# Sliding-window attention beside a gated MLP: the order of the first chunk's transposes and V projections

## The chip, the cores and the metric

The kernel runs on one core of a Trainium2 chip. The metric is the device time of one execution in microseconds, lower is better. The engines are called PE (matrix multiply; PEld is its weight load, which overlaps it), DVE (vector), ACT (scalar, activations), POOL and SP (here only an issuer of DMAs).

## The reference

For x of shape (1, 2048, 512), all in bf16:

```python
xn = _layernorm(x)                              # (x - mean) / sqrt(var + 1e-5) over the 512
return x + _A_ref(xn, wqkv, wo) + _B_ref(xn, w_gate, w_up, w_down)

# _A_ref: 32 heads of 16; each query sees itself and the 255 keys before it
qkv = (xn @ wqkv).reshape(B, S, 3, H, Dh)
p = softmax(where(mask, q @ k.T * Dh ** -0.5, -1e9))
A = (p @ v) @ wo
# _B_ref: F = 1792
B = ((xn @ w_gate) * (xn @ w_up)) @ w_down
```

## The kernel before

The 2048 rows are worked on in four chunks T of four blocks of 128 rows. For a chunk, the rows are normalised (`norm_stats`, `norm_scale`, `norm_apply`), transposed so that the 512 inputs lie on the partitions (`norm_transpose`, tile `xnT`, four groups of 128 inputs, index k), and projected to V (`proj_v`, L243), to Q and K (`proj_qk`, L255) and to gate and up (L399, L410). Scores (L317), exponentials (L323), masks, P times V (L370), the down projection and Wo follow, and the gate, up and down matmuls of one chunk are spread by `run` between the attention steps. The program writes out the order of every engine by hand: each engine runs its instructions in the order in which `run` records them, and waits on semaphores where it needs another's result.

The change touches what happens before that steady part. `setup` issues the loads on SP in a written order: x of blocks 0, 1 and 2 to 3, then `Wqkv` in three DMAs (the V columns, then K, then Q), then `Wg`, `Wu`, x of blocks 4 to 7, the second halves of `Wg` and `Wu`, `Wd`, `Wo`, and x of the blocks left. Then `keep_busy(40)` puts 40 matmuls of zeros (tile `wps`, L131) on PE.

`first_chunk` normalises chunk 0. DVE computes the statistics (L173, L174), POOL the inverse root (L186), DVE scales a block to `xn` (L194). PE transposes the block's four 128x128 parts (L213) into a PSUM tile `xTp`, and ACT copies that to `xnT` (L214): for block 0 in two PSUM tiles of two parts, each copied by itself, for the other blocks in one tile of four parts and one copy. `proj_v(b)` is four matmuls of 128x512 that sum over k into one PSUM bank `vp`; DVE or ACT then copies it to V (L236, L234). `ps_m` is a pool of four PSUM banks, from which `xTp`, `vp`, `qkp` and also the idle matmuls take theirs.

PE's order in the first chunk is: the transposes of block 0, eight idle matmuls, the transposes of block 1, the V sum of block 0, the transposes of block 2, the V sum of block 1, the transposes of block 3, the V sums of blocks 2 and 3, and then the first K, Q and K sums (L255). So each block's transposes stand one whole V sum ahead of the sum that reads them.

Of the kernel before, what the change touches and what calls it, by code (L numbers as in the profile page):

```python
# [8 lines left out]
F32 = mybir.dt.float32  # L9
I32 = mybir.dt.int32  # L10
ACT = mybir.ActivationFunctionType
ALU = mybir.AluOpType
# [22 lines left out]
class Kernel:  # L35
# [26 lines left out]
    def setup(self):  # L62
        nc, const, NT, NF = self.nc, self.const, self.NT, self.NF
        self.x = const.tile([128, NT, 512], BF16, name="x")
        self.Wqkv = const.tile([128, 4, 1536], BF16, name="Wqkv")
        self.Wo = const.tile([128, 4, 512], BF16, name="Wo")
        self.Wg = const.tile([128, 4, self.F], BF16, name="Wg")
        self.Wu = const.tile([128, 4, self.F], BF16, name="Wu")
        self.Wd = const.tile([128, NF, 512], BF16, name="Wd")
        xv = self.x_d.rearrange("(t p) d -> p t d", p=128)  # L70
        wq = self.w_d["qkv"].rearrange("(k p) n -> p k n", p=128)
        wg = self.w_d["g"].rearrange("(k p) n -> p k n", p=128)
        wu = self.w_d["u"].rearrange("(k p) n -> p k n", p=128)
        for lo, hi in ((0, 1), (1, 2), (2, 4)):
            nc.sync.dma_start(out=self.x[:, lo:hi, :], in_=xv[:, lo:hi, :])
        for lo in (1024, 512, 0):
            nc.sync.dma_start(out=self.Wqkv[:, :, lo:lo + 512], in_=wq[:, :, lo:lo + 512])
        h = self.F // 2
        for lo in (0, h):
            nc.sync.dma_start(out=self.Wg[:, :, lo:lo + h], in_=wg[:, :, lo:lo + h])  # L80
            nc.sync.dma_start(out=self.Wu[:, :, lo:lo + h], in_=wu[:, :, lo:lo + h])
            if lo == 0:
                nc.sync.dma_start(out=self.x[:, 4:8, :], in_=xv[:, 4:8, :])
        nc.sync.dma_start(out=self.Wd[:], in_=self.w_d["d"].rearrange("(f p) n -> p f n", p=128))
        wo = self.w_d["o"].rearrange("(c p) n -> p c n", p=128)
        for c in range(4):
            nc.sync.dma_start(out=self.Wo[:, c, :], in_=wo[:, c, :])
        for lo, hi in ((8, 10), (10, 12), (12, NT)):
            nc.sync.dma_start(out=self.x[:, lo:hi, :], in_=xv[:, lo:hi, :])

        warm = const.tile([128, 1], F32, name="warm")
        nc.vector.memset(warm[:], 0.0)
        nc.scalar.activation(out=warm[:], in_=warm[:], func=ACT.Exp)
        self.idle = const.tile([128, 128], BF16, name="idle")
        nc.vector.memset(self.idle[:], 0.0)
        self.keep_busy(40)
        ident = const.tile([128, 128], BF16, name="ident")
        nc.gpsimd.memset(ident[:], 0.0)
        nc.gpsimd.affine_select(out=ident[:], in_=ident[:], compare_op=ALU.not_equal, fill=1.0,
                                base=0, pattern=[[-1, 128]], channel_multiplier=1)  # L100
        self.ident = ident
        pi = const.tile([128, 1], I32, name="pi")
        nc.gpsimd.iota(pi[:], pattern=[[0, 1]], base=0, channel_multiplier=1)
        podd = const.tile([128, 1], I32, name="podd")
        nc.vector.tensor_scalar(out=podd[:], in0=pi[:], scalar1=4, scalar2=1,
                                op0=ALU.arith_shift_right, op1=ALU.bitwise_and)
        self.odd = const.tile([128, 1], F32, name="odd")
        nc.vector.tensor_copy(out=self.odd[:], in_=podd[:])
        self.even = const.tile([128, 1], F32, name="even")
        nc.vector.tensor_scalar(out=self.even[:], in0=self.odd[:], scalar1=-1.0, scalar2=1.0,  # L110
                                op0=ALU.mult, op1=ALU.add)
        self.mhalf = const.tile([128, 4], F32, name="mhalf")
        nc.gpsimd.memset(self.mhalf[:], -0.5)
        self.diag = const.tile([128, 64], BF16, name="diag")
        self.far = const.tile([128, 64], BF16, name="far")
        nc.gpsimd.memset(self.diag[:], BIG)
        nc.gpsimd.memset(self.far[:], BIG)
        for half in (slice(0, 64), slice(64, 128)):
            self.triangle(self.diag[half], True)
            self.triangle(self.far[half], False)  # L120
        self.xnT, self.Q, self.hT, self.OT = {}, {}, {}, {}
        self.K, self.V, self.VS = {}, {}, {}
        self.strips, self.parts, self.at = {}, {}, {}
        self.stock = []
        self.new_values()

    def keep_busy(self, n):

        ps = self.ps_m.tile([128, 128], F32, tag="M", name="wps")
        for _ in range(n):  # L130
            self.nc.tensor.matmul(ps[:], lhsT=self.idle[:], rhs=self.idle[:], start=True, stop=True)  # L131

    def new_chunk(self, T):

# [55 lines left out]
    def norm_apply(self, t):  # L190
        nc = self.nc
        mv, j, rs = self.stats.pop(t)
        xn = self.work.tile([128, 512], BF16, tag="xn", name="xn")
        nc.vector.tensor_scalar(out=xn[:], in0=self.x[:, t, :], scalar1=mv[:, j, 0:1],  # L194
                                scalar2=rs[:, j:j + 1], op0=ALU.subtract, op1=ALU.mult)
        self.book("dve", MASK)
        self.xns[t] = xn

    def norm_transpose(self, t, by_dma):

        nc = self.nc
        xn = self.xns.pop(t)
        T, b = divmod(t, 4)
        if b == 0:
            self.xnT[T] = self.chunk2.tile([128, 4, 4, 128], BF16, tag="xnT", name=f"xnT{T}")
        if by_dma:
            nc.sync.dma_start_transpose(out=self.xnT[T][:, b, :, :], in_=xn[:])
            return
        n = 2 if b == 0 else 4
        for lo in range(0, 4, n):  # L210
            ps = self.ps_m.tile([128, n, 128], BF16, tag="M", name="xTp")
            for k in range(n):
                nc.tensor.transpose(ps[:, k, :], xn[:, 128 * (lo + k):128 * (lo + k) + 128], self.ident[:])  # L213
            nc.scalar.activation(out=self.xnT[T][:, b, lo:lo + n, :], in_=ps[:], func=ACT.Copy)  # L214

    def bank(self, ks, name):

# [54 lines left out]
    def first_chunk(self):  # L272

        self.new_chunk(0)
        for b in range(2):
            self.norm_stats(b, 1)
            self.norm_scale(b, 1)
        for b in (0, 1, 2):
            self.norm_apply(b)
            if b < 2:  # L280
                self.norm_stats(b + 2, 1)
                self.norm_scale(b + 2, 1)
        self.norm_transpose(0, False)
        self.keep_busy(8)
        for b in range(4):
            if b < 3:
                self.norm_transpose(b + 1, False)
            self.proj_v(b, engine="act" if b == 2 else "dve")
            if b == 0:
                self.norm_apply(3)  # L290
        self.proj_qk(0, 0, 1, engine="dve")
        self.proj_qk(0, 0, 0, engine="act")
        self.swap_halves(0, self.nc.scalar)
        self.proj_qk(0, 1, 1, engine="dve")
# [234 lines left out]

    def run(self):  # L530
        self.xns, self.stats, self.sums = {}, {}, {}
        self.pads = 0
        self.now, self.free = 0, dict(act=0, dve=0)
        self.setup()
        NCH = self.NCH
# [17 lines left out]
        spent, n = 0, 0  # L553
# [62 lines left out]
        T = NCH - 1  # L616
# [58 lines left out]
```

The softmax here doesn't subtract the row's maximum and nothing guards it: scores larger than these inputs give would overflow.

## Time and profile before

| what | value |
|---|---|
| median of 5 runs | 263.36 us (263.25 to 264.04) |
| the profiled execution | 263.37 us, its span 261.3 us |
| PE busy | 255.5 us, 98% of the span |
| DVE, ACT, POOL busy | 179.5, 176.4, 115.7 us |
| first transposes; first V matmul; first Q/K sum | 5.25; 6.67; 10.77 us from the start of the span |
| `Wqkv`: three DMAs of 512 KB, issue to landing | 4.3, 5.7 and 6.6 us |

In the views of the profile a row of the timeline gives start and length in us, engine, line, operation, out<-in, and in brackets the idle time of the engine before it with what ended it. Rows of equal instructions are merged (x4), and a few per cent of the matmul records can be missing.

### The profile page before, as it was taken

The page shows a single profiled execution, that of the slowest core. Times are in us where ns is not written, and L with a number is a line of the kernel's source. Part 1 is how long each engine was busy: PE and PEld are TensorE (multiplying, and loading weights), DVE is VectorE, ACT ScalarE, POOL GpSimd, SP SyncE. Part 2 cuts the span into 40 slices and gives each one's busy share as a digit, 9 for nine tenths or more (in the row PEclk, how much of TensorE's full clock was granted, in tenths as well). Part 3 has the DMA queues.
Part 4 walks back from the last instruction along what each step waited for, and adds up shares of the span by engine and source line. Part 5 has one row for each costly group of instructions (what it writes and reads, how often), then busy time and mean ns, then how long its engine had stood idle before and what let it go on. Part 6 is the DMA issues. An engine that isn't in the chain of part 4 may idle for free.

```text
span 261.3 us, 7718 instructions
## 1 busy us (share of the span) xinstructions
PE 255.5 (98%) x3154; PEld 117.5 (45%) x3170; DVE 179.5 (69%) x357; ACT 176.4 (67%) x143; POOL 115.7 (44%) x278
## 2 busy tenths in 40 slices
PE   7999999999999999999999999999999999999995
PEld 7444444444344544444544454444544445444453
DVE  6787888779846597557974769767794235977344
ACT  3477688888757776678775567777787546787500
POOL 6225342425457644333457644534443451464600
PEclk9999999999999999999999999999999999999999
DMA  6999910120011300002001310001000100000002
GB/s 199 376 352 340 283 29 20 24 48 1 3 38 26 102 3 1 3 0 48 3 3 40 84 43 3 0 1 32 20 3 4 39 21 25 3 0 3 1 3 83
DMA packets 19427, 15.05 MB, mean 58 GB/s; under 512 B 7360, under 2 KB 19392, under 8 KB 19392
## 3 DMA queue, kind: packets, MB, share of 16 engines
q1 hardware_dynamic: 18848, 14.26, 19.0%
q8 instruction: 26, 0.43, 0.7%
q10 hardware_dynamic: 544, 0.30, 0.4%
q14 instruction: 9, 0.07, 0.1%
HBM read 9.70 MB, written 2.10 MB: 45 GB/s over the span
## 4 chain that ended last, share of the span: by engine, by line
PE 96%; DVE 1%; DMA 1%; issue 1%
PE gp L399 19%; PE up L410 19%; PE psd L432 17%; PE qkp L255 11%; PE S L317 10%; PE acc L370 7%; PE vp L243 5%; PE psd L438 5%; PE L L432 2%; DMA x<-in_A_x_dram 1%; DVE st L173 1%; PE L L438 1%; PE L L370 0%; PE xTp L213 0%; DVE xn L194 0%
## 5 line engine op out<-in xcount | busy, mean ns | idle before, releaser
L323 ACT ACTIVATE P<-S 128x2048 bf16<-128x2048 f32 x75 | 140.7, 1876 | 49.6 <-PE S L317 41.0
L162 POOL TENSOR_SCALAR_AFFINE_SELECT P<-P 64x256 bf16<-64x256 bf16 x224 | 99.4, 444 | 124.1 <-ACT P L323 108.9
L399 PE MATMUL gp<-xnT,Wg 128*128 128x512 bf16 x224 | 60.1, 380 | 0.0
L410 PE MATMUL up<-xnT,Wu 128*128 128x512 bf16 x224 | 59.1, 380 | 0.0
L415 DVE TENSOR_TENSOR hT<-up,gsb 128x512 bf16<-128x512 f32 x56 | 38.3, 685 | 18.4 <-PE up L410 13.1
L432 PE MATMUL psd<-Wd,hT 128*128 128x512 bf16 (+1 forms) x202 | 46.9, 369 | 0.8 <-issue 0.6
L347 DVE TENSOR_TENSOR P<-P,diag 128x512 bf16<-128x512 bf16 (+1 forms) x75 | 29.6, 394 | 5.9 <-ACT P L323 5.9
L432 PEld LDWEIGHTS <-hT 128*128 128x128 bf16 x238 | 21.3, 98 | 25.3 <-issue 3.5
L410 PEld LDWEIGHTS <-Wu 128*128 128x128 bf16 x224 | 20.4, 98 | 25.6 <-issue 3.3
L399 PEld LDWEIGHTS <-Wg 128*128 128x128 bf16 x224 | 20.3, 98 | 25.3 <-issue 3.3
L317 PE MATMUL S<-Q,K 32*128 32x320 bf16 (+4 forms) x720 | 29.8, 254 | 0.1
L255 PE MATMUL qkp<-xnT,Wqkv 128*128 128x512 bf16 x128 | 29.9, 380 | 0.0
L234 ACT ACTIVATE gsb<-gp 128x512 bf16<-128x512 f32 x38 | 22.3, 596 | 7.7 <-PE gp L399 6.9
L317 PEld LDWEIGHTS <-K 32*128 32x128 bf16 x720 | 10.2, 92 | 30.7 <-issue 30.3
L376 DVE STREAM_TRANSPOSE at<-acc 128x512 f32<-128x512 f32 x30 | 19.1, 688 | 6.5 <-PE acc L370 6.4
L448 DVE TENSOR_TENSOR x<-psd,x 128x512 bf16<-128x512 f32 (+1 forms) x15 | 9.7, 655 | 15.7 <-PE psd L438 15.7
L255 PEld LDWEIGHTS <-Wqkv 128*128 128x128 bf16 x128 | 11.7, 98 | 14.7 <-issue 1.8
L370 PE MATMUL acc<-P,VS 64*32 64x320 bf16 (+4 forms) x672 | 17.7, 253 | 0.0
L370 PE MATMUL acc<-P,V 64*32 64x320 bf16 (+4 forms) x672 | 17.5, 253 | 0.0
L370 PEld LDWEIGHTS <-V 64*32 64x32 bf16 x720 | 15.1, 91 | 2.3 <-issue 1.7
L243 PE MATMUL vp<-Wqkv,xnT 128*128 128x512 bf16 x60 | 14.9, 380 | 0.3 <-issue 0.2
L370 PEld LDWEIGHTS <-VS 64*32 64x32 bf16 x720 | 14.7, 91 | 0.6 <-issue 0.2
(54 smaller groups left out, 179.2 us busy)
## 6 DMA issues: line engine op xcount, KB each, us to landing
out_dram<-x SPq DMA_DIRECT2D x15, 128.0 KB, 1.9
Wg<-in_B_w_gate_dram SPq DMA_DIRECT2D x2, 896.0 KB, 11.0
Wu<-in_B_w_up_dram SPq DMA_DIRECT2D x2, 896.0 KB, 12.4
Wd<-in_B_w_down_dram SPq DMA_DIRECT2D x1, 1792.0 KB, 17.3
Wqkv<-in_A_wqkv_dram SPq DMA_DIRECT2D x3, 512.0 KB, 5.7
x<-in_A_x_dram SPq DMA_DIRECT2D x2, 512.0 KB, 8.9
VS<-V SPq DMA_DIRECT2D x6, 144.0 KB, 2.6
x<-in_A_x_dram SPq DMA_DIRECT2D x3, 256.0 KB, 6.7
```

The lines of the kernel that those rows point to most:

```text
L162: nc.gpsimd.affine_select(out=v, in_=v, pattern=pattern + [[1 if diag else -1, 64]], compare_op=ALU.is_ge if diag else ALU.is_gt, fill=0.0 ...
L234: nc.scalar.activation(out=out, in_=in_, func=ACT.Copy)
L243: nc.tensor.matmul(ps[:], lhsT=self.xnT[T][:, b, k, :], rhs=self.Wqkv[:, k, 1024:1536], start=(k == 0), stop=(k == 3))
L255: nc.tensor.matmul(ps[:], lhsT=self.Wqkv[:, k, lo:lo + 128], rhs=self.xnT[T][:, :, k, :], start=(k == 0), stop=(k == 3))
L317: nc.tensor.matmul(S[:, e, col:col + n], lhsT=self.K[U, c][rows, keys], rhs=self.Q[T, c][rows, q:q + n], start=True, stop=True, tile_posit ...
L323: nc.scalar.activation(out=P[:, :, 0:col], in_=S[:, :, 0:col], func=ACT.Exp, scale=0.25)
L347: self.nc.vector.tensor_tensor(out=v, in0=v, op=ALU.min, in1=self.diag.unsqueeze(1).unsqueeze(1).to_broadcast([128, 4, n, 64]))
L370: nc.tensor.matmul(accs[par][32 * e:32 * e + 32, q:q + n], lhsT=v, rhs=P[rows, e, col:col + n], start=(i == 0), stop=(i == len(todo) - 1), ...
L399: nc.tensor.matmul(ps[:], lhsT=self.Wg[:, k, 128 * f:128 * f + 128], rhs=self.xnT[T][:, :, k, :], start=(k == 0), stop=(k == 3))
L410: nc.tensor.matmul(ps[:], lhsT=self.Wu[:, k, 128 * f:128 * f + 128], rhs=self.xnT[T][:, :, k, :], start=(k == 0), stop=(k == 3))
L415: nc.vector.tensor_tensor(out=self.hT[T, f][:], in0=ps[:], in1=self.gsb[:], op=ALU.mult)
L432: nc.tensor.matmul(ps, lhsT=self.hT[T, f][:, 128 * b:128 * b + 128], rhs=self.Wd[:, f, c0:c1], start=(f == 0), stop=False)
```

## The change

Block 0's scaling is issued as two instructions of 256 columns. The copies from `xTp` to `xnT` are all of two parts (128x256), also where `xTp` holds four. The V columns of `Wqkv` come in two DMAs, input rows 0 to 255 (k 0 and 1) and rows 256 to 511 (k 2 and 3), and x of blocks 8 to 11, two DMAs before, is one. The idle matmuls write to the PSUM tile that the scores use later, and there are two and two in place of eight. PE's order becomes: transposes of block 0, two idle matmuls, k 0 to 2 of V of block 0, transposes of block 1, k 3 of block 0, two idle matmuls, k 0 and 1 of block 1, transposes of block 2, k 2 and 3 of block 1, k 0 and 1 of block 2, transposes of block 3, k 2 and 3 of block 2, and the V sum of block 3. The engine that evacuates each V sum stays the same.

```diff
-        for lo in (1024, 512, 0):
-            nc.sync.dma_start(out=self.Wqkv[:, :, lo:lo + 512], in_=wq[:, :, lo:lo + 512])
+        for lo, ks in ((1024, slice(0, 2)), (1024, slice(2, 4)), (512, slice(0, 4)), (0, slice(0, 4))):
+            nc.sync.dma_start(out=self.Wqkv[:, ks, lo:lo + 512], in_=wq[:, ks, lo:lo + 512])
...
-        for lo, hi in ((8, 10), (10, 12), (12, NT)):
+        for lo, hi in ((8, 12), (12, NT)):
             nc.sync.dma_start(out=self.x[:, lo:hi, :], in_=xv[:, lo:hi, :])
...
     def keep_busy(self, n):
 
-        ps = self.ps_m.tile([128, 128], F32, tag="M", name="wps")
+        if self.spare is None:
+            self.spare = self.s_tiles.tile([128, 4, 512], F32, tag="S", name="wps")
         for _ in range(n):
-            self.nc.tensor.matmul(ps[:], lhsT=self.idle[:], rhs=self.idle[:], start=True, stop=True)
+            self.nc.tensor.matmul(self.spare[:, 0, 0:128], lhsT=self.idle[:], rhs=self.idle[:], start=True, stop=True)
...
-        nc.vector.tensor_scalar(out=xn[:], in0=self.x[:, t, :], scalar1=mv[:, j, 0:1],
-                                scalar2=rs[:, j:j + 1], op0=ALU.subtract, op1=ALU.mult)
+        n = 256 if t == 0 else 512
+        for lo in range(0, 512, n):
+            nc.vector.tensor_scalar(out=xn[:, lo:lo + n], in0=self.x[:, t, lo:lo + n], scalar1=mv[:, j, 0:1],
+                                    scalar2=rs[:, j:j + 1], op0=ALU.subtract, op1=ALU.mult)
...
-            nc.scalar.activation(out=self.xnT[T][:, b, lo:lo + n, :], in_=ps[:], func=ACT.Copy)
+            for k in range(0, n, 2):
+                nc.scalar.activation(out=self.xnT[T][:, b, lo + k:lo + k + 2, :], in_=ps[:, k:k + 2, :], func=ACT.Copy)
...
         self.norm_transpose(0, False)
-        self.keep_busy(8)
-        for b in range(4):
-            if b < 3:
-                self.norm_transpose(b + 1, False)
-            self.proj_v(b, engine="act" if b == 2 else "dve")
-            if b == 0:
-                self.norm_apply(3)
+        self.keep_busy(2)
+        self.proj_v(0, (0, 1, 2))
+        self.norm_transpose(1, False)
+        self.proj_v(0, (3,), engine="dve")
+        self.keep_busy(2)
+        self.norm_apply(3)
+        self.proj_v(1, (0, 1))
+        self.norm_transpose(2, False)
+        self.proj_v(1, (2, 3), engine="dve")
+        self.proj_v(2, (0, 1))
+        self.norm_transpose(3, False)
+        self.proj_v(2, (2, 3), engine="act")
+        self.proj_v(3, engine="dve")
```

More of the change, by code (lines that the diff above doesn't have):

```diff
@@ L531, in run @@
         self.xns, self.stats, self.sums = {}, {}, {}
-        self.pads = 0
+        self.pads, self.spare = 0, None
         self.now, self.free = 0, dict(act=0, dve=0)
```

## The prediction

> **What bounds the kernel now.** I read the page first, then the clock and busy time by stretches of the first chunk, then the table of PE's waits, then the timeline of the first 11 us, then the transfers of `Wqkv`.
>
> The page's first and fourth part:
>
> ```profile
> PE 255.5 (98%) x3154; PEld 117.5 (45%) x3170; DVE 179.5 (69%) x357; ACT 176.4 (67%) x143; POOL 115.7 (44%) x278
> ...
> PE 96%; DVE 1%; DMA 1%; issue 1%
> ```
>
> PE is busy for 98% of the span and is 96% of the chain that ended last. Whatever stands ahead of PE's unbroken stretch is therefore paid once, in full. Where the stretch begins is read from the busy time in stretches (columns: length, PE, PEld, DVE, ACT, POOL busy with instruction counts, clock, DMA share, GB/s) and from PE's own waits (us in total, times, longest):
>
> ```profile
> 5.20:6.44 1.24, 0.90 (x16) 0.68 (x13) 1.21 (x4) 0.66 (x2) 0.99 (x3) 1.00 1.04 354
> 6.44:10.77 4.33, 4.28 (x28) 2.00 (x29) 2.79 (x6) 2.39 (x4) 1.50 (x4) 1.00 1.07 374
> 10.77:29.00 18.23, 18.23 (x123) 7.44 (x121) 14.54 (x29) 12.15 (x10) 5.67 (x18) 1.00 1.08 350
> ```
>
> ```profile
> PE psd L432 <- issue: 0.6, 4, 0.2
> PE xTp L213 <- DVE xn L194: 0.3, 1, 0.3
> ```
>
> From 10.77 on PE never pauses (18.23 of 18.23), and its only wait for another engine behind the start is the 0.3 us for `xn` at 6.44. So the change is worth exactly what it does to the moment at which the first Q/K sum (L255) starts, 10.77 now. The timeline up to there (start, length, engine, line):
>
> ```profile
> 4.81 0.38 DVE L194 TENSOR_SCALAR xn<-x,mv,rs 128x512 bf16<-128x512 bf16 x1
> ...
> 5.25 0.40 PE L213 MATMUL xTp<-ident,xn 128*128 128x128 bf16 x4
> ...
> 5.57 0.66 ACT L214 ACTIVATE xnT<-xTp 128x256 bf16<-128x256 bf16 x2 [3.29 <-PE xTp L213]
> ...
> 6.44 0.40 PE L213 MATMUL xTp<-ident,xn 128*128 128x128 bf16 x4 [0.34 <-DVE xn L194]
> ...
> 6.87 0.60 ACT L214 ACTIVATE xnT<-xTp 128x512 bf16<-128x512 bf16 x1 [0.64 <-PE xTp L213]
> ...
> 9.04 1.89 PE L243 MATMUL vp<-Wqkv,xnT 128*128 128x512 bf16 x8
> ...
> 9.89 0.55 PEld L243 LDWEIGHTS <-xnT 128*128 128x128 bf16 x4 [0.32 <-ACT xnT L214]
> ```
>
> Prices from it: one V matmul 0.216 us (1.73 from 9.04 to 10.77, over 8); four transposes 0.235 of PE's time; from the first transpose of a block to the start of its copy 0.43 (6.44 to 6.87); a copy of 128x256 0.38, and a second one behind it starts 0.28 later (0.66 for two); from a copy's end to PE 0.05 (the copy of block 3 runs 9.24 to 9.84, its weight load comes at 9.89). In the order of before, the four V matmuls (0.86) of the block before lie behind each block's transposes, and the copy ends under them.
>
> The `Wqkv` transfers:
>
> ```profile
> L77 SPq DMA_DIRECT2D Wqkv<-in_A_wqkv_dram x3: 469/507/507, 2.2 to 3.2; - x3
> ...
> DMA to landing us min/median/max: 4.3/5.7/6.6
> ```
>
> The first (V) is issued at 2.18 and lands 4.3 later, at 6.48; its first user starts at 6.67, so today the weights just miss being late.
>
> **The change part by part.**
>
> Scaling in halves. A 128x512 scaling lasts 0.38 and lets the next DVE instruction start after 0.30 (4.81 to 5.11); a 128x1 one of the same kind (L183) lasts 0.15 and takes 0.07. Half way: 0.27 and 0.185. The first half is done at 5.08, but the 40 idle matmuls hold PE to 5.20, so the first pair of transposes gains 0.05. The second half ends at 5.27, and everything behind it on DVE (statistics of block 2, `xn` of block 1, then 2 and 3) slips by 0.07: `xn` of block 1 is ready for PE at 6.51 instead of 6.44. The two copies of block 0, already halves, start at 5.52 and 5.80, and PE can use them at 5.95 and 6.23.
>
> Fewer idle matmuls. Eight at 0.056 become two; PE then stands for 0.4 us until 5.95. In front of a wait, that costs nothing. The other two lie in the first bubble below. Their PSUM moves to the score tile, whose first use is at 13.46: nothing.
>
> Three of block 0's V matmuls go ahead of block 1's transposes. They could run from 5.95 to 6.60 (3 x 0.216), in time that is idle now. But the third reads input rows 256 to 383, which come with the second of the two V transfers. The same bytes end where they end now, 6.48, at the earliest; the first half, half way between the landing of `x` (4.83: issue 1.71, 3.1 to land) and 6.48, comes at 5.66 and is in time for 5.95. For the boundary between two transfers there is no row of its own. From below: it costs nothing, and the third matmul waits for the data it waits for anyway, or, if the second half landed by 6.3, not at all. From above: `x`'s third transfer took 1.5 us for 256 KB after the one before it, against 0.83 per half of V. That one met an empty queue (61 to 138 GB/s between 2.8 and 3.6 us, 340 to 390 from 4.6 on), so I stay near V's own row and take 6.55. The third matmul then starts at 6.57, and block 1's transposes, queued behind it on PE, at T = 6.57 + 0.22 = 6.79; never before 6.60.
>
> A page speaks against the second DMA. "DMA: Bandwidth & Descriptors" (section "Anatomy of one DMA") gives each DMA of the GpSimd path a fixed part of about 2.0 us. The rows here (the K weights, issued at 2.7, land 5.7 later at 8.4, 1.9 us after V, for 512 KB) show it hidden by a queue that never empties; paid in series it would put the second half near 8.5 and the sum, by an estimate from that page, some 2 us later.
>
> V sums split around the transposes, copies in halves. Now only two V matmuls (0.43) follow block 2's and block 3's transposes before a sum that needs those transposes. The copy of the first half waits for all four transposes (in the built program the first half's copy waits for the count after the fourth, and the second half's for nothing), so it starts 0.43 after the first transpose, as before, and the next V matmul comes 0.43 + 0.38 + 0.05 = 0.86 after it. PE has only 0.235 + 0.43 = 0.67 to do: a bubble of 0.19, twice. For block 1 it has 0.235 + 0.216 + 0.11 of idle matmuls: a bubble of 0.30, once. The second halves are ready 0.28 later, under the first pair's 0.43. `xn` of blocks 2 and 3 is ready at 7.69 and about 8.88, the transposes want it at T + 1.29 = 8.08 and 9.37: no wait. The V evacuations keep the same engines and have over 1 us to spare.
>
> So each block takes 0.86 + 0.43 = 1.29. Block 2's transposes start at T + 1.29, block 3's at T + 2.58, the last four V matmuls at T + 3.44, the first Q/K sum at T + 4.30. Before it was 6.44 + 4.33. The three matmuls moved ahead save 0.65 and the two old waits for `xn` 0.17; the bubbles give 0.68 back and the two idle matmuls 0.11: the interval stays, and what is left is the start of block 1's transposes, 6.79 against 6.44. First Q/K sum: 6.79 + 4.30 = 11.09, that is 0.32 us later.
>
> The other DMAs. One more issue (0.5 us) stands on SP ahead of the K and Q weights, `Wg`, `Wu` and `x` of blocks 4 to 7, but their data queue behind the same bytes. K lands at 8.4 for 10.77, Q at 9.8 for 11.63, `Wg` at 12.3 for 18.55. The merged transfer of `x` blocks 8 to 11 takes one issue off at 24 us, first used at 71.5. Nothing, with 1.8 us or more of cover. Behind 10.77 every engine's order is the same.
>
> **The sum.** The profiled execution took 263.37 (span 261.3, 2.07 around it), the median of the runs is 263.36. 263.37 + 0.32 = 263.69 us, slower by 0.12%. A measurement of this kernel can tell about 0.2%, or 0.53 us, from no change.
>
> **The rivals.**
>
> Slower by more than 0.2%: the second V transfer. The third matmul blocks PE in order, so each 0.1 us that it lands later is 0.1 us on the end; from 6.76 (0.21 later than I take) the change passes 0.53 us. At 6.95 it gives 264.1; at the far bound of 1.5 us per half (4.83 + 1.5 + 1.5 = 7.83) 264.97. For it: the weights just miss being late now, and the last of V's bytes are what is asked for. Against: the queue is full there.
>
> Slower by the clock: idle matmuls follow each other at 0.107 us up to about 5.1 and at 0.056 from then on. If the gaps at 5.55 and 7.3 keep or bring back the slow rate to about 8.5, seven V matmuls cost 0.2 more each, less what the bubbles hide: about 1 us, 264.7. Against it: the rate rose under the 40 idle matmuls, which stay.
>
> Faster: no bubbles. If the V matmuls ran without a pause from 5.95 on, 16 x 0.216 + 3 x 0.235 + 0.11 puts the first Q/K sum at 10.22: 0.55 us gained, 262.82. It needs the copies' latency gone, and no row gives that. With the second half early (T = 6.60) and bubbles half as long, it is no change, 263.2.
>
> **How the numbers follow.** Forecast (T from 6.60 to 7.0, three bubbles) 0.73, giving 263.50 to 263.90; late weights 0.17; clock 0.05; shorter bubbles 0.05. The range takes the forecast with 0.15 below it for somewhat smaller bubbles and for the spread of the runs, and the nearer half of the late weights: 263.35 to 264.1. Faster by over 0.2%: 0.03, of the shorter bubbles; slower: 0.22, late weights and clock; within: 0.75.
>
> **What would show it.** In the profile after: block 1's transposes near 6.8 behind three V matmuls, the third waiting for a DMA; V matmuls waiting 0.3, 0.2 and 0.2 for ACT's `xnT`; L255 starting at 11.1; nothing different behind it. Transposes of block 1 at 6.5, or copies that start after two transposes, would prove the sum wrong on the fast side; a wait of V matmuls for `Wqkv` over 0.4 us on the slow side.

## The result, and the profile after

| | before | after |
|---|---|---|
| median | 263.38 us (40 runs, 263.11 to 264.1) | 264.99 us (21 runs, 263.63 to 267.05) |
| ratio | 1 | 1.0063, 95% [1.0052, 1.0073] |
| profiled execution | 263.37 us, span 261.3 | 267.05 us, span 265.0 |

The change makes the kernel 0.63% slower, about 1.6 us. The forecast was 263.69, its range 263.35 to 264.1; the result lies outside, on the side of the rival "late weights". The profiled execution is the slowest of the 21. It is read for where the time goes; sizes over all runs come from the medians and ratios.

The page of the changed kernel, first and fourth part. PE has as much work as before, but a share of the chain has gone to DMA and to "issue":

```profile
PE 255.6 (96%) x3150; PEld 116.8 (44%) x3166; DVE 179.7 (68%) x358; ACT 176.4 (67%) x146; POOL 115.9 (44%) x278
...
PE 95%; DMA 2%; issue 1%; SPq 1%; ACT 0%; DVE 0%
```

Busy time in the same stretches as before. In the second, PE was busy for 4.28 of 4.33; now for 2.87:

```profile
5.20:6.44 1.24, 1.10 (x8) 0.43 (x7) 1.21 (x5) 0.66 (x2) 0.81 (x2) 1.00 0.69 187
6.44:10.77 4.33, 2.87 (x22) 1.55 (x23) 2.77 (x6) 1.32 (x4) 1.49 (x3) 1.00 1.00 353
10.77:29.00 18.23, 18.19 (x124) 7.38 (x122) 13.36 (x27) 12.54 (x13) 5.15 (x16) 1.00 1.08 353
```

PE's waits name the place, one wait of 1.3 us of a V matmul for the weights. They also show a second thing, of which the prediction knew nothing, an idle time without a releaser ("issue") ahead of P times V (L380):

```profile
PE vp L247 <- DMA Wqkv<-in_A_wqkv_dram: 1.3, 1, 1.3
...
PE acc L380 <- issue: 0.2, 1, 0.2
```

The timeline of PE (start, length, line, tiles; in brackets the idle time and what ended it):

```profile
5.80 0.60 PE L247 MATMUL vp<-Wqkv,xnT 128*128 128x512 bf16 x2
7.66 0.38 PE L247 MATMUL vp<-Wqkv,xnT 128*128 128x512 bf16 x1 [1.25 <-DMA Wqkv<-in_A_wqkv_dram]
7.87 0.38 PE L216 MATMUL xTp<-ident,xn 128*128 128x128 bf16 x4
...
8.73 0.61 PE L247 MATMUL vp<-Wqkv,xnT 128*128 128x512 bf16 x2
9.17 0.39 PE L216 MATMUL xTp<-ident,xn 128*128 128x128 bf16 x4
...
12.21 1.03 PE L259 MATMUL qkp<-xnT,Wqkv 128*128 128x512 bf16 x4
```

Two V matmuls run at 5.80 on the first half of the weights, which landed at 5.34. The third waits until the second half lands, at 7.61, and block 1's transposes, behind it in PE's order, start at 7.87 where the forecast had 6.79. From there to the first Q/K sum it is 4.34 us.

Compared row by row with before, everything is 1.45 us late from the first Q/K sum on. This stays exactly so until about 125 us, where PE's weight loads stop for half a microsecond in the middle of a dense burst:

```profile
126.73 0.10 PEld L380 LDWEIGHTS <-VS 64*32 64x32 bf16 x3 [0.50 <-issue]
```

From there on everything is 1.87 us late, up to the last matmul. The span is longer by 3.65, though: the other 1.78 came at the very end, where SP waits for the last store, which landed 3.33 us after its issue (1.54 before). SP's waits for the stores, before and after:

```profile
SPq L670 <- DMA out_dram<-x: 0.9, 4, 0.3
```

```profile
SPq L680 <- DMA out_dram<-x: 2.8, 2, 2.4
```

So there are three losses: late weights, a pause without a releaser, and sometimes a late end. The late end has two forms. In the profiled execution it lies inside the span, and the execution ends 2.05 us behind the span as usual. In 5 of the other 20 runs the end lies 2.4 to 3.4 us behind the span; otherwise it is 2.0 to 2.3, and 2.0 to 2.2 in the runs of the kernel before. Whether both have one cause is open.

### The profile page after: what moved, and what is told of

It is laid out like the page before. It is cut to its first block, busy times and chain, and to the rows that moved or that the text cites. A ratio compares the mean times of both kernels' runs of the same rounds, so it can differ in the third digit from the quotient of the medians.

```text
span 265.0 us, 7713 instructions
## 1 busy us (share of the span) xinstructions
PE 255.6 (96%) x3150; PEld 116.8 (44%) x3166; DVE 179.7 (68%) x358; ACT 176.4 (67%) x146; POOL 115.9 (44%) x278
## 4 chain that ended last, share of the span: by engine, by line
PE 95%; DMA 2%; issue 1%; SPq 1%; ACT 0%; DVE 0%
PE gp L409 19%; PE up L420 19%; PE psd L442 17%; PE qkp L259 11%; PE S L327 9%; PE acc L380 7%; PE vp L247 5%; PE psd L448 5%; PE L L442 2%; DMA Wqkv<-in_A_wqkv_dram 2%; PE L L448 1%; PE L L380 0%; SPq L75 0%; PE xTp L216 0%; SPq L77 0%
## 5 line engine op out<-in xcount | busy, mean ns | idle before, releaser
L380 PE MATMUL acc<-P,VS 64*32 64x320 bf16 (+4 forms) x672 | 17.9, 253 | 0.2 <-issue 0.2
L380 PE MATMUL acc<-P,V 64*32 64x320 bf16 (+4 forms) x672 | 17.7, 253 | 0.0
L247 PE MATMUL vp<-Wqkv,xnT 128*128 128x512 bf16 x60 | 15.5, 380 | 1.9 <-DMA Wqkv<-in_A_wqkv_dram 1.3
L380 PEld LDWEIGHTS <-V 64*32 64x32 bf16 x720 | 15.0, 91 | 2.3 <-issue 1.7
L380 PEld LDWEIGHTS <-VS 64*32 64x32 bf16 x720 | 14.7, 91 | 1.1 <-issue 0.7
```

The lines of the kernel that those rows point to most:

```text
L247: nc.tensor.matmul(ps[:], lhsT=self.xnT[T][:, b, k, :], rhs=self.Wqkv[:, k, 1024:1536], start=(k == 0), stop=(k == 3))
L380: nc.tensor.matmul(accs[par][32 * e:32 * e + 32, q:q + n], lhsT=v, rhs=P[rows, e, col:col + n], start=(i == 0), stop=(i == len(todo) - 1), ...
```

## The experiments

The empty instructions and idle matmuls that some kernels add change no data. "Shift" is the start of the first Q/K sum in the profiled execution against 10.77; "last V piece" is the landing of the last of V's weights there (not resolved in e9's trace); "count" is the number of PE's instructions in the built program. Shift and landing are those of one execution each, median and ratio those of all runs.

| run | median, us | ratio, 95% | last V piece | shift | count |
|---|---|---|---|---|---|
| changed kernel | 264.99 | 1.0063 [1.0052, 1.0073] | 7.61 | +1.45 | 6600 |
| e1 V split only | 263.65 | 1.0012 [1.0003, 1.0021] | 7.34 | +0.27 | 6609 |
| e2 V whole | 264.62 | 1.0054 [1.0042, 1.0066] | 6.38 | +0.64 | 6600 |
| e3 and copies whole | 265.10 | 1.0075 [1.0056, 1.0093] | 7.32 | +2.22 | 6600 |
| e4 third matmul behind | 264.13 | 1.0040 [1.0024, 1.0056] | 6.69 | +0.42 | 6600 |
| e5 old order, V first | 269.54 | 1.0231 [1.0218, 1.0244] | 4.80 | +2.80 | 6661 |
| e6 new order, V first | 270.17 | 1.0269 [1.0244, 1.0293] | 4.97 | +2.86 | 6652 |
| e7 old order, V on ACT | 266.39 | 1.0115 [1.0099, 1.0131] | 6.26 | +3.87 | 6609 |
| e8 one ahead, V on ACT | 266.11 | 1.0115 [1.0088, 1.0141] | 5.11 | +1.42 | 6596 |
| e9 four idle fewer | 263.44 | 1.0002 [0.9994, 1.0011] | - | +0.09 | 6601 |
| e10 nine empty at start | 265.25 | 1.0063 [1.0048, 1.0079] | 8.16 | +1.99 | 6609 |
| e11 V whole, nine at start | 264.26 | 1.0037 [1.0024, 1.0049] | 7.15 | +1.41 | 6609 |
| e12 one ahead, 13 at start | 263.71 | 1.0009 [1.0001, 1.0018] | 6.45 | -0.10 | 6609 |
| e13 old order, V first, 40 idle | 268.64 | 1.0197 [1.0164, 1.0229] | 4.90 | +5.49 | 6609 |
| e14 new order, V first, 40 idle | 267.02 | 1.0148 [1.0118, 1.0178] | 4.81 | +5.76 | 6609 |
| e15 old order, V in four | 263.67 | 1.0011 [1.0002, 1.0020] | 6.88 | -0.01 | 6609 |
| e16 nine in the gaps | 264.25 | 1.0038 [1.0026, 1.0050] | 7.29 | +1.13 | 6609 |
| e17 V whole, nine in the gaps | 264.01 | 1.0017 [1.0007, 1.0027] | 6.40 | +0.66 | 6609 |
| e18 third behind, nine in the gaps | 263.63 | 1.0010 [0.9998, 1.0022] | 6.93 | +0.22 | 6609 |

**One part at a time (e1 to e4).** e1 is the kernel before with the split of V's transfer alone; e2 is the changed kernel without it; e3 is e2 with one copy for four transposes; e4 is the changed kernel with the third V matmul behind block 1's transposes.

```diff
e1  -for lo in (1024, 512, 0):
    +for lo, ks in ((1024, slice(0, 2)), (1024, slice(2, 4)), (512, slice(0, 4)), (0, slice(0, 4))):
e2  the reverse, in the changed kernel
e3  e2, and
    -for k in range(0, n, 2):
    -    nc.scalar.activation(out=self.xnT[T][:, b, lo + k:lo + k + 2, :], in_=ps[:, k:k + 2, :], func=ACT.Copy)
    +nc.scalar.activation(out=self.xnT[T][:, b, lo:lo + n, :], in_=ps[:], func=ACT.Copy)
e4  -self.proj_v(0, (0, 1, 2))              +self.proj_v(0, (0, 1))
    -self.proj_v(0, (3,), engine="dve")     +self.proj_v(0, (2, 3), engine="dve")
```

> The kernel before with one edit: the V columns of Wqkv come in two DMAs (input rows 0 to 255, 256 to 511). Theory S (splitting the transfer is itself what makes its second half late): the second half lands near 7.6 as in the changed kernel, the third V matmul of block 0 waits for it, the first Q/K sum starts about 0.35 to 0.5 us later than 10.77, the time is 263.7 to 263.9. Theory O (the lateness comes with the rest of the change): the second half lands near 6.5, the time stays at 263.4.

> The changed kernel with V's columns in one DMA as before, all else as changed. Theory S: the transfer lands near 6.5, block 0's three V matmuls run from there, block 1's transposes start at 7.15, the first Q/K sum 4.3 to 4.35 later at about 11.5; the time is 0.7 us over before, 264.1, and the wide spread of the changed kernel's runs goes. Theory O: V lands after 7 here too, the time stays at about 265.

> As the changed kernel with V in one DMA, and the copies of blocks 1 to 3 whole (128x512) as before. If the bubbles behind the transposes are the copy's latency, each block's first V matmul now comes 0.43 + 0.60 + 0.05 = 1.08 after its transposes instead of 0.86, so three times 0.22 is added to the kernel with halved copies: about 264.75, 0.65 over it. If the bubbles are set by something else (weights, xn), nothing is added.

> The changed kernel with the V matmul of k = 2 of block 0 moved behind block 1's transposes, next to k = 3; V still in two DMAs. Theory S: the transposes start at 6.51, but the two matmuls of the second half then wait to 7.6; blocks 2 and 3 follow from there, the first Q/K sum at about 11.6, the time 264.2, under the changed kernel by 0.6 to 0.8. If the late weights cost because they stand ahead of the transposes alone, it comes to 263.4 or less.

Neither the split in the old order (1.0012) nor the new order without the split (1.0054) gives the whole 1.0063. e2 took 0.5 us more than theory S gave it (264.62 against 264.1), though its first Q/K sum came at 11.41, near the 11.5 of the forecast; what it lost behind that is the subject of e9 to e17. In e1 the second half landed late too, at 7.34, but the old order has block 1's transposes ahead of the matmuls that need it. e3 shows what the copies in halves are worth: in its timeline PE waits 0.26 to 0.36 us for the copy ahead of each block's V matmuls, where the changed kernel's table of PE's waits has no row of that kind, and a block takes 1.51 us in place of 1.30:

```profile
9.08 0.60 PE L246 MATMUL vp<-Wqkv,xnT 128*128 128x512 bf16 x2 [0.36 <-ACT xnT L217]
...
10.60 0.60 PE L246 MATMUL vp<-Wqkv,xnT 128*128 128x512 bf16 x2 [0.26 <-ACT xnT L217]
```

From block 1's transposes to the first Q/K sum e3 takes 4.98 us, the changed kernel and e2 4.34. The rest of e3's shift is V, which as a whole landed at 7.32 here and at 6.38 in e2: one transfer, the same order of issue, almost a microsecond of scatter.

**V early (e5 to e8).** To see the new order without late weights, V was loaded ahead of x (e5, e6, with 66 idle matmuls to bridge the wait for x) or on ACT's queue (e7, e8). e8 also has another order: one V matmul ahead of the next block's transposes and three behind.

```diff
e5  before:   +nc.sync.dma_start(out=self.Wqkv[:, :, 1024:1536], in_=wq[:, :, 1024:1536])   (ahead of x)
              -for lo in (1024, 512, 0):      +for lo in (512, 0):
              -self.keep_busy(40)             +self.keep_busy(66)
e6  the same in the changed kernel, in place of its split
e7  before:   +nc.scalar.dma_start(out=self.Wqkv[:, :, 1024:1536], in_=wq[:, :, 1024:1536])
              -for lo in (1024, 512, 0):      +for lo in (512, 0):
e8  as e7, in the changed kernel, and in its order
              proj_v(b, (0,)), norm_transpose(b + 1), proj_v(b, (1, 2, 3)); no second group of idle matmuls
```

> The kernel before with the V columns (one DMA) loaded ahead of x instead of behind it, and 66 idle matmuls at the start instead of 40 to bridge the longer wait for x. V can't be late; x lands about 1.4 us later and the whole first chunk with it: about 264.7, 1.4 over before. It is the base for the next one. Theory W (the wait for V's weights makes nearly all of the changed kernel's loss) and its rival, theory B (the new order loses by itself, by bubbles), expect the same here.

> The changed kernel with V's columns in one DMA ahead of x, and 66 idle matmuls, as in the kernel with the old order and V first. Theory W: with no wait for weights block 1's transposes start behind three V matmuls, 0.07 to 0.17 later relative to x's landing than in the old order, and the interval from there to the first Q/K sum is 4.3 against 4.33: 0.05 to 0.2 us over the old order with V first, and a spread of runs as narrow. Theory B: at least 0.6 over it.

> The kernel before with the V transfer issued on ACT's queue, ahead of its table load at 0.8, instead of on SP behind x. If SP's row of issues (0.45 us each) leaves the transfer engines idle between x's pieces, V fills these holes and lands near 5, with x's first block late by 0.1 to 0.4: the time goes up by that, 263.3 to 263.7. If the two queues only share the bytes, x's first block lands up to 0.4 later and V at 5 to 5.5. If the queues disturb each other, V lands at 6.5 or later.

> The changed kernel with V in one DMA on ACT's queue, and one V matmul instead of three moved ahead of each block's transposes, so that three (0.65) lie behind them over the copy's latency: k 0 of block b, transposes of b + 1, k 1 to 3 of block b. By the arithmetic of the prediction no bubble is left (0.235 + 0.65 against 0.86) and the interval from block 1's transposes to the first Q/K sum shrinks from 4.33 to 3.95: 0.3 to 0.4 less than the old order with V on ACT's queue, if V is there by 6.

Their times don't answer the question. e7 and e8 are no test of the order: with V on ACT's queue x of block 1, which lands at 3.35 in the changed kernel, landed at 6.62 and 5.49. e5 and e6 do answer it, in their first stage. With V early the first Q/K sum starts at 13.57 in the old order (first row) and at 13.63 in the new one:

```profile
13.57 0.60 PE L256 MATMUL qkp<-xnT,Wqkv 128*128 128x512 bf16 x2
...
13.63 0.59 PE L260 MATMUL qkp<-xnT,Wqkv 128*128 128x512 bf16 x2
```

So without late weights the new order costs about 0.06 us; this is one execution of each, and x of blocks 0 and 1 landed 0.1 later in e6. But e5 was to take 264.7 and took 269.54: 2.80 from x, which now comes behind V, and 3.7 behind the first Q/K sum, in two pauses inside dense bursts of P times V, of which this is the first:

```profile
95.76 0.29 PE L371 MATMUL acc<-P,V 64*32 64x256 bf16 x3 [1.56 <-issue]
```

Like the 0.5 us of the changed kernel it is idle time without a releaser, at other places and larger. What the kernels that pause have in common is that the number of PE's instructions is not that of the kernel before. The page's third part shows 26 blocks of 16 KB loaded during the run ("q8 instruction: 26"); they are taken for PE's, since their times move with its count. The kernel before holds groups of empty instructions on PE (27:110 and 57:150 in its table `PADS`). In the trace the block that starts at 120.1 us before starts at 124.0 in the changed kernel, that is at some 122.6 with the 1.45 of shift taken off, close to the dense burst of P times V, which starts at 123.35 before. So a theory F was formed: a change of PE's instruction count moves the loads of instructions against the dense bursts, and PE runs dry.

**The instruction count (e9 to e12).** e9 takes four idle matmuls from the kernel before and does nothing else; e10 to e12 bring the count of changed kernels back to 6609 with empty instructions at PE's start.

```diff
e9  before:  -self.keep_busy(8)     +self.keep_busy(4)
e10 changed: +for _ in range(9): nc.tensor.nop("pad", nofuse=True)    (ahead of keep_busy(40))
e11 the same in e2
e12 13 of them in e8's order, V as a whole on SP
```

> The kernel before with four of the eight idle matmuls between the transposes of blocks 0 and 1 left out, nothing else: 8 PE instructions fewer (6601 against 6609; the changed kernel has 6600). The start can't gain or lose by it. Theory F (the place of PE's instruction blocks of 16 KB moves against its dense stretches, and PE runs out of instructions near 125 us): a pause of 0.1 to 0.45 near 125 us, some runs with a late end, 263.6 to 263.9. Rival (the pause comes from the changed start or from the DMAs): 263.4, no pause.

> The changed kernel with 9 empty PE instructions at the very start (PE waits there anyway), so that from the first scores on every PE instruction has the same number as in the kernel before. Theory F: no pause near 125 us and no late end; what is left is the late second half of V, 1.0 to 1.45 us at the first Q/K sum: 264.3 to 264.8, under the changed kernel by 0.2 to 0.45. Rival: unchanged, 265.0.

> The changed kernel with V in one DMA and the 9 empty PE instructions: the new order and the halves alone. By the arithmetic of the prediction with V landing at 6.4 to 6.5: first Q/K sum 0.65 to 0.75 later, 264.0 to 264.1. If V lands at 6.9 in most runs: 264.5.

> One V matmul instead of three ahead of each block's transposes, three behind them; V in one DMA on SP, 13 empty PE instructions so that the numbering is that of the kernel before. By the arithmetic, with V landing at 6.4: block 1's transposes at 6.65, no bubbles, the first Q/K sum 3.95 later at 10.6, 0.15 earlier than before: 263.2. With V at 6.9: 11.1, 0.3 later, 263.7.

Fewer idle matmuls cost nothing by themselves (1.0002). For e9 theory F was wrong: with 6601 instructions in the old order there was no pause and, in 11 runs, no late end. So a smaller count alone is not enough. The times of the block say more. With the shift of each execution taken off, its packet ends at 121.1 to 121.6 us in the twelve kernels with 6609 (the kernel before among them), at 122.2 in e9, and at 123.2 to 123.8 in the five with 6596 or 6600. Of these five, e2 (123.2) shows no pause there, e4 (123.6) one of 0.06 us, and e3, the changed kernel and e8 (123.7 to 123.8) 0.44, 0.42 and 0.39. The later the block, the longer the pause, and none where it is there before the burst.

In e10 to e12 pause and late ends were gone, but e10's median was no better than that of the changed kernel (265.25). Nine empty instructions at the start put the idle matmuls from 1.07 to 1.6 us, and the first transposes came at 5.78 in e10 and 5.42 in e11 (5.04 in the changed kernel); the second half of V landed at 8.16 in e10's profiled execution. That start was a bad place for them: the same nine where PE idles (e16, e17) make it 264.25 and 264.01, against 265.25 and 264.26.

**Which share is whose (e13 to e18).** e13 and e14 repeat e5 and e6 with 40 idle matmuls and a count of 6609; e15 splits V in four in the old order; e16 puts the nine empty instructions where PE idles in any case; e17 and e18 are e16 with V in one transfer, and with the third V matmul behind block 1's transposes.

```diff
e13 e5 with keep_busy(40);   e14 e6 with keep_busy(40) and nine empty instructions at the start
e15 before:  +for lo, ks in [(1024, slice(k, k + 1)) for k in range(4)] + [(512, slice(0, 4)), (0, slice(0, 4))]:
e16 changed: +five empty instructions behind the first keep_busy(2), four behind the second
e17 e16 with for lo in (1024, 512, 0);   e18 e16 with proj_v(0, (0, 1)) and proj_v(0, (2, 3))
```

> The kernel before with the V weights' transfer issued ahead of x, the first 40 idle matmuls left as they are and so 6609 instructions on TensorE, as in the kernel before. The V weights then land before any normalised block exists, so that the first stage waits for x alone; it is the partner of the next run. Theory F (instruction fetches pause TensorE only where the count of its instructions was changed): no pause behind the first Q/K sum; that sum starts some 2.8 us later than the 10.77 of the kernel before, as it did with 66 idle matmuls, and the time is 263.4 + 2.8 = 266.2, against 269.5 with 66. Rival (the pauses of 1.8 and 1.9 us come from loading V first, not from the instruction count): they stay, and the time is 269 to 270.

> The changed kernel with the V weights in one transfer ahead of x, 40 idle matmuls, and nine empty instructions at TensorE's start, which bring its count to 6609. Against its partner it differs by the new order of V matmuls, the halves of the first block and the four idle pairs, with no late V weights and no change of the instruction count. Theory W (the new order loses by weights that land late, since a third V matmul stands ahead of the transposes): without late weights it costs its bubbles alone, so the first Q/K sum starts 0.05 to 0.2 us behind the partner's, and the time is the partner's plus 0.05 to 0.2, 266.3 to 266.5. Rival B (the order is dear by itself, by its bubbles at the copies): plus 0.6 or more, at least 266.8.

> The kernel before, in its own order of matmuls, with the V weights in four transfers of 128 input rows each in place of one; 6609 instructions on TensorE. Two transfers gave a second half at 7.34 in the profiled execution and a ratio of 1.0012. Theory S (each further boundary between transfers puts the last piece later): the last quarter lands at 8.0 or later, K and Q behind it, and the time is 264.2 to 264.9. Rival (the landing scatters from execution to execution, and the number of transfers has little to do with it): the last quarter lands between 6.4 and 7.4, and the time is 263.3 to 263.8.

> The changed kernel with nine empty instructions on TensorE, five behind the first group of idle matmuls between V sums and four behind the second, where TensorE has idle time ahead of it; the count is 6609 again, and the start is not delayed, as it was with the nine at the start (265.25). Theory F (of the changed kernel's loss up to 0.44 us is a pause of TensorE in an instruction fetch near 125 us, and the scattered late last store goes with it): no pause at 125, no execution whose end lies more than 2.3 us behind its span, and 264.4 to 264.8. Rival (the pause has to do with the shift in time and not with the count): unchanged, 265.0, with the pause in the profile.

> The changed kernel with the V weights in one transfer and the nine empty instructions in TensorE's idle stretches, 6609 instructions: it differs from the run that measured 264.25 (1.0038) by the second V transfer alone. Theory S2 (halves land their last piece later than one transfer by some 0.7 us in this order, and each 0.1 of lateness is paid): 263.5 to 263.9, and the first V matmul starts when the whole lands, at 6.4 to 7.3. Rival O (the order itself, with a third V matmul ahead of block 1's transposes, pays for any landing behind 6.4, and the split gives back by its early first half what its late second half costs): 264.1 to 264.5, the same as with the split within 0.25 us.

> The changed kernel with its third V matmul of block 0 moved behind block 1's transposes, as in the order before, with the nine empty instructions in the idle stretches, 6609 instructions; the split stays. Without the nine it measured 264.13 (1.0040). Theory W (a late second half is paid in full since the third V matmul stands ahead of the transposes): the transposes start at about 6.8 whether or not the second half is there, and the time is 263.5 to 263.8, 0.5 to 0.7 below the 264.25 of the changed order. Rival (the third matmul's place does not matter, the two that wait for the second half behind the transposes lose the same): 264.1 to 264.4.

e13 and e14 answer F and miss the rest: 268.64 and 267.02 against 266.2 and 266.3 to 266.5. The shift of the first Q/K sum holds to the last matmul within 0.01 us in both (+5.49 and +5.48; +5.76 and +5.75): no pause, in the arrangement that paused twice with 6661 and 6652. But with only 40 idle matmuls ahead of an x that lands later, the granted clock (third column from the end) fell back to half. e13's stretches:

```profile
4.00:7.40 3.40, 0.86 (x15) 0.69 (x12) 1.85 (x6) 0.00 (x0) 0.55 (x1) 1.00 0.99 342
7.40:14.20 6.80, 5.54 (x28) 3.24 (x29) 3.59 (x9) 1.85 (x4) 2.63 (x6) 0.50 1.04 362
```

So they say nothing on the cost of the order, and e5 and e6 remain the evidence for that.

e16 is the clean test of F. With the count restored and nothing delayed, the shift of +1.13 holds to the last matmul (+1.12), no run in nine ends late, and the median is 264.25. PE's waits no longer have a row for P times V, and SP's last wait is as before:

```profile
PE vp L247 <- DMA Wqkv<-in_A_wqkv_dram: 0.8, 1, 0.8
PE xTp L216 <- DVE xn L197: 0.2, 1, 0.2
```

```profile
SPq L684 <- DMA out_dram<-x: 0.9, 3, 0.4
```

The ratio goes from 1.0063 to 1.0038: 0.0025 of 263.4, or 0.66 us, went with the instruction count. Two more pairs differ by the nine empty instructions alone: e2 and e17 (1.0054 to 1.0017, 0.97 us), e4 and e18 (1.0040 to 1.0010, 0.79). Over the changed kernel and its variants, 11 of 44 runs with 6596 or 6600 instructions end more than 2.3 us behind their span, and none of 61 with 6609.

e18 then moves one matmul and goes from 1.0038 to 1.0010, 0.74 us. In e16 block 1's transposes (L216) stand behind the third V matmul, which waits:

```profile
7.34 0.38 PE L247 MATMUL vp<-Wqkv,xnT 128*128 128x512 bf16 x1 [0.82 <-DMA Wqkv<-in_A_wqkv_dram]
7.55 0.38 PE L216 MATMUL xTp<-ident,xn 128*128 128x128 bf16 x4
```

In e18 the second half landed at 6.93, later than the 6.55 of the forecast too, but the transposes no longer wait for it. It cost 0.24 us there (1.54 from block 1's transposes to block 2's, in place of 1.30); behind a third matmul, by the 0.26 and 4.34 of the changed kernel, the same landing would have put the first Q/K sum 0.76 later than before, in place of 0.22:

```profile
6.41 0.40 PE L216 MATMUL xTp<-ident,xn 128*128 128x128 bf16 x4
6.97 0.38 PE L247 MATMUL vp<-Wqkv,xnT 128*128 128x512 bf16 x1 [0.17 <-DMA Wqkv<-in_A_wqkv_dram]
```

e17 leaves the third matmul ahead and takes V in one transfer: 1.0017, that is 0.55 us less than e16. Theory W (e18) is upheld; for the split, the truth lies between the two expectations of e17: medians 0.24 us apart, ratios 0.55.

e15 speaks against a cost of each boundary between transfers. In its profiled execution four pieces landed at 5.31, 6.23, 6.58 and 6.88, where theory S had 8.0 or later for the last, and the ratio is that of two pieces. Over the profiled executions with V on SP behind x, V as a whole landed at 6.38, 6.40, 6.45, 6.49, 7.15 and 7.32 (e2, e17, e12, before, e11, e3), the second of two halves at 6.69, 6.93, 7.29, 7.34, 7.61 and 8.16 (e4, e18, e16, e1, changed, e10). Second halves are later, by 0.85 between the medians, and all six are later than the forecast's 6.55; but the two sets overlap. In the changed kernel's profiled execution it is the rate that fell: between 4 and 8 us its DMA engines moved less than those of the kernel before (transfers of the changed kernel, then of the kernel before):

```profile
DMA packets 1095, 1.07 MB, mean 268 GB/s; under 512 B 49, under 2 KB 1095, under 8 KB 1095
```

```profile
DMA packets 1365, 1.36 MB, mean 339 GB/s; under 512 B 41, under 2 KB 1365, under 8 KB 1365
```

Over these executions the rate is 268 to 309 GB/s with halves and 300 to 339 with V whole. Why it falls (e15's is 278 with four pieces and an early last one, e17's 300 with V whole), and so why second halves are late, is open. No run beat the kernel before; the best changed order, e12, is 1.0009.

## Why the prediction was wrong, step by step

- **The second half of V lands at 6.55: wrong, the failing step.** It landed at 7.61 in the profiled execution, and in the others with two halves between 6.69 and 8.16. The forecast took V's own row, one landing at 6.48, for the place where the bytes end, added 0.07 for the boundary, and called the queue full. 6.48 was a usual landing for one transfer: four of six lie at 6.38 to 6.49, the other two at 7.15 and 7.32. It was not that of a second half, whose median is 7.3. So in the sum it is the wait of the third matmul ahead of the transposes that was too small: it was priced at 0.32 us (T at 6.79), and taking it away gave 0.74 (e16 to e18). The far bound of 7.83 was in the text, but all late weights together had only 0.17.
- **Each 0.1 us that the second half is late is 0.1 us on the end: right**, and it makes the step above expensive. Landing to transposes is 0.26 in the changed kernel and in e16 (7.29 to 7.55), forecast 0.24. e18 shows the other side: behind the transposes a late second half cost 0.24 us. The prediction saw the mechanism; it priced it from one landing of another transfer.
- **"Behind 10.77 every engine's order is the same", "nothing different behind it", and fewer idle matmuls cost nothing: wrong in effect.** The order is the same, and e9 confirms the price of the idle matmuls themselves. But eight of PE's instructions fewer for them, and one wait less, moved the loading of instructions; with the late ends this is 0.66 us (e16) that no term of the sum held. That restoring the count wins such an amount back is shown by e16, e17 and e18, each against its partner; e9 shows that a smaller count does not cost in every case. That the load is late for the burst near 125 us is inferred from the times of its packet, which order the pauses: 0.42 us in the changed kernel, 0.06 in e4, none in e2, with the same count. How the late ends come about is open.
- **The bubbles of 0.30, 0.19 and 0.19: right.** From block 1's transposes to the first Q/K sum: 4.30 forecast, 4.34 measured; from block to block 1.29 forecast, 1.30 and 1.31 measured; transposes to V matmul 0.86 and 0.86. The table of PE's waits has no row for them, unlike the forecast's sign, because a matmul counts as busy to its modelled end; the starts show them. That the copies in halves are what holds the bubbles down is shown by e3 (4.98).
- **The first half at 5.66, the first V matmul at 5.95: a little early in fact,** 5.34 and 5.80. It gains nothing, as forecast, since the third matmul waits.
- **Scaling in halves delays `xn` of block 1 by 0.07: not seen.** e18's transposes of block 1 start at 6.41, before at 6.44.
- **The clock rival: not the cause here.** In the changed kernel's profiled execution the idle matmuls follow each other at 0.056 us from 3.9 on (0.107 ahead of it), and the granted clock is 1.00 in all stretches shown. It did take over in e7, e13 and e14. The step to the fast pace comes at another time in each execution, though, and that is part of the scatter of the shifts: in e1 and e4 the idle matmuls of the first stage still run at the slow pace (eight in 1.06 us, before in 0.61; two in 0.42, in the changed kernel in 0.28), and block 1's transposes start at 6.59 and 6.84, against 6.44 before and 6.41 in e18.
- **A fixed part per transfer, paid in series: no.** "The Trainium skill", page "DMA: Bandwidth & Descriptors" (section "Anatomy of one DMA"), of which the forecast wrote that it would put the second half near 8.5, has that price for the GpSimd path. The second, third and fourth piece in e15 landed 0.92, 0.35 and 0.30 us behind the one before, so no such part stands in series between transfers on SP's queue here, as the forecast took it. The lateness is not this.

The sum as the runs have it, in parts of 263.4 us: 1.66 lost; 0.66 of it to the instruction count; 0.74 to the third matmul's place ahead of the transposes, waiting for a late second half (e16 to e18); 0.26 left in e18, whose profiled execution loses 0.24 to the second half behind the transposes. By the intervals of the table each part is known to some 0.4 us. That the 0.26 is near the 0.32 of the forecast is chance: that stood for the third matmul's place. The split's own share lies inside the 0.74: undoing it alone gives 0.55 (e16 to e17). The scaling in halves, the other PSUM tile of the idle matmuls and the merged transfer of x were not run by themselves; e18 has all three.

## What to carry to other kernels

A matmul that is moved ahead of others on an in-order engine makes all of them pay for its latest operand, so its price is the spread of that landing. One trace shows one sample of it, and of the transfer as it was, not of its half; ask for a margin of the spread, here about a microsecond. What waits for a transfer goes behind what doesn't, as in e18. And in a kernel whose engine is busy to 98%, the number of its instructions can matter: here a few matmuls taken out at the start cost time a hundred microseconds later, and a control with the count restored by empty instructions in idle stretches told this apart.

## What the runs showed of the hardware

- **A dense PE can pause with the count of its instructions changed.** Nine or 13 instructions fewer: up to 0.44 us in the burst near 125 us, and a late end in a quarter of the runs. 43 or 52 more: two pauses of 1.8 to 2.0 us near 91 and 188 us of the old time. With 6609: none in any profiled execution, but for two of 0.2 to 0.3 us in e7 that were made up again. That a late block of instructions is behind the pause near 125 us is inferred from the times of its packet in 18 executions; for the pauses of e5 and e6 it is not shown.
- **The clock falls back on part-time work.** In e13 the granted clock went from 1.00 to 0.50 after a stretch of 3.4 us in which PE was busy for 0.86, and stayed there for 6.8 us; so it did in e14 after 3.41 us with 1.68 of work, and in e7, for 3.4 us, after 3.41 with 0.91. "The Trainium skill", page "TensorE: Matmul & The Clock Gate" (section "Part 1: The HAM clock gate"), has a free-running window of about 3.4 us after which an idle engine is slowed. The length agrees; here a window that was busy for a quarter, or for half, still ended in the slow rate.
- **A transfer on a second queue holds back those on the first.** V's weights on ACT's queue put the landing of x of block 1 from 3.35 to 6.62 us (e7) and to 5.49 (e8).
